# Attention ahead of an MLP and a mixture of experts: transposes by VectorE in squares of 32, value products with the keys' weights stationary, fronts three heads ahead

## The chip, the cores and the metric

The kernel runs on one core of one Trainium2 chip, as one program. The metric is the device time of one execution in microseconds; the profile's own clock counts from the start of its span. Engines are named as in the profile: PE is TensorE's stream of matmuls, PEld its loads of weights, DVE is VectorE, ACT is ScalarE, POOL is GpSimd, SP is SyncE, which here only issues DMAs.

## The reference

Softcapped attention over 2 batches of 12 heads with 448 tokens and 64 columns, then a squared-ReLU MLP over 896 tokens, then a mixture of 8 experts of which each token takes one:

```python
scores = scale * np.matmul(q, k.transpose(0, 1, 3, 2))
scores = cap * np.tanh(scores / cap)
scores = scores - np.max(scores, axis=-1, keepdims=True)
attn = np.exp(scores)
attn = attn / (np.sum(attn, axis=-1, keepdims=True) + 1e-09)
x = np.matmul(attn, v)              # then heads side by side: 896 x 768
...
h = x @ w_in                        # 768 x 2048
r = np.maximum(h, 0.0)
x = (r * r) @ w_out                 # 2048 x 768
...
expert_idx = np.argmax(xn @ en.T / tau, axis=1)
for e in range(E):                  # 8 experts, 768 x 1024 x 768
    mask = expert_idx == e
    h = np.maximum(x[mask] @ w1[e], 0.0)
    out[mask] = gate_w[mask, None] * (h @ w2[e])
```

The scores are not shifted by their maximum in the kernel; their cap of 30 bounds the exponential.

## The kernel before, in words

**Tiling.** Activations are kept transposed: partitions hold columns of the model, the free dimension the 448 tokens of a batch. A batch's tokens are cut into 4 blocks of 112 (`NC`, `CP`); token 4p + c stands in block c at place p. A head has 64 columns (`D`), so two heads, a pair, fill 128 partitions.

**Precision.** A float32 operand of the large products is written as the sum of two float32r parts, hi (rounded) and lo (the rest), and a product takes three passes: hi x hi, lo x hi, hi x lo (`pass3`, L450 to L452). Scores do it with stacked halves: `k_r` holds k twice beside each other, so that its transpose `kp` has k in both halves of the partitions; `kh` and `kl` are its hi and lo part. `q_s` holds q's hi part beside its lo part, so its transpose `q2` has q hi in partitions 0 to 63 and q lo in 64 to 127. Two passes of 128 partitions then make all products of a block of keys: kh with q2, and kl with q2. The products of p_t with v are plain float32, of which one product is two instructions in the trace.

**A head.** `front_k(n)` (GpSimd makes the hi and lo part of q in rows, L312 and L313; four transposes by TensorE, L317; a copy from PSUM, L320 by VectorE or L322 by ScalarE; a subtraction by VectorE, L324) and `front_q(n)` (four transposes by TensorE, L331; a copy from PSUM, L334 or L336) prepare k and q. `scores(n, hf)` makes half of the scores: for two blocks of keys two passes into a PSUM bank of 448 queries (L345, L346) and a tanh by ScalarE out of that bank (L347), then one exp over both (L348); `p_t` has keys on partitions and queries in the free dimension. `values(n)` makes four float32 products (L358): the weights are a block's 112 keys by 64 columns of v beside 64 columns of ones (`vt`), the moving operand is p_t with 448 queries. So one half of the bank `pv` receives the values, transposed as they are wanted, and the other half the sum over the keys, in 64 equal rows; ScalarE adds the guard and brings the sums to `den` (L367). `finish(m)`, for a pair of heads, takes the reciprocal of den (128 x 448, L386), multiplies (L389, twice) and leaves to `split_pair` the hi part `xh` by ScalarE (L383) and the lo part `xl` by VectorE (L384).

**Order.** The program is written as Python generators; every engine executes its own instructions in the order in which they were written, and waits for others by semaphores. The generator `attention()` goes through 24 heads. In its loop over n it writes: front_k(n+2), scores(n+1, 0), front_q(n+2), scores(n+1, 1), the conversion of a weight block, finish of the pair before, values(n). In the first batch (heads up to 12 of the loop) it runs alone: three banks take turns for scores, three for values, and `convert_early` makes VectorE turn four blocks of w_in from float64 to float32 along the way (L263, L169, L170, L172; a block every other head). Then `interleave(mlp(0), 192, att, ATN)` weaves it into the first MLP of batch 0: after every step of the MLP (three passes) as many steps of attention as `ATN` over 192 asks for. There two banks serve scores, two values, and two the MLP; the copies of `front_k` and `front_q` go to ScalarE (`eng["kh"]`). After that come the MLP of batch 1 with the router of batch 0, the experts, and one tile of tokens that were left over.

**Loads.** `load_head` is called for two heads ahead of the loop and once in every front_k. It issues k twice (into the two halves of k_r) and q on SP; `load_v` issues v of head n+2 after values(n). Pools give every tile a few buffers (k_r and q_r 2, p_t 4); a writer waits until the readers of the buffer's last use are done.

Of the kernel before, what the change touches and what calls it, by code (L numbers as in the profile page):

```python
# [8 lines left out]
F32 = mybir.dt.float32  # L9
# [4 lines left out]
ALU = mybir.AluOpType  # L14
# [6 lines left out]
def kernel(  # L21
# [37 lines left out]
    T = 64  # L59
    OOB = 4096.0  # L60
# [16 lines left out]
    # ---------------------------------------------------------------- heads  # L77
# [3 lines left out]
    vt = [ap.tile([CP, NC, 2, D], F32, tag=f"vt{i}", name=f"vt{i}", bufs=1) for i in range(2)]  # L81

    def load_head():
        n = nload[0]
        if n >= len(order):
            return
        nload[0] = n + 1
        b, h = order[n]
        q_r = ap.tile([CP, NC, D], F32, tag="q_r", name=f"q_r{n}", bufs=2)
        k_r = ap.tile([CP, NC, 2, D], F32, tag="k_r", name=f"k_r{n}", bufs=2)  # L90
        kk = k[b, h].rearrange("(p c) d -> p c d", c=NC)
        qq = q[b, h].rearrange("(p c) d -> p c d", c=NC)
        e = nc.sync if n else nc.scalar
# [3 lines left out]
        raw[n] = (q_r, k_r)  # L97

    def load_v(n):
        b, h = order[n]  # L100
        nc.sync.dma_start(vt[n % 2][:, :, h % 2, :], v[b, h].rearrange("(p c) d -> p c d", c=NC))
# [4 lines left out]
    # ------------------------------------------------------------ constants  # L106
# [6 lines left out]
    identr = const.tile([P, P], F32R, name="identr")  # L113
    nc.vector.tensor_copy(identr, ident)
    for i in range(2):
        nc.gpsimd.memset(vt[i][:, :, 1 - i, :], 1.0)
# [13 lines left out]
    # ------------------------------------------------------- weight streams  # L130
# [949 lines left out]
```

## Time and profile before

| | |
|---|---|
| runs of the kernel | 540.63, 540.63, 2953.97 us; median 540.63 |
| span of the profiled execution, within one of such time | 536.6 us |
| between the span and the median | 4.0 us |
| busy: PE, PEld | 520.5 us (97%), 439.6 us (82%) |
| busy: DVE, ACT, POOL | 388.2 us (72%), 308.1 us (57%), 39.2 us (7%) |
| instructions | 7614 |
| DMA | 87.88 MB in 110713 packets, 163 GB/s over the span |

The profile shows one execution. Busy time of an engine is the time in which at least one of its instructions ran. TensorE overlaps: a matmul is in flight while the next begins, so the length of one matmul is longer than the distance to the next, and the distance between starts tells the pace. In a row `xN` says how many instructions it stands for. A row ends with the idle time of the engine just before it and with what ended that. Shapes stand as partitions x elements, for matmuls as the weights' partitions*columns and then the moving operand.

### The profile page before, as it was taken

The page shows a single profiled execution, that of the slowest core. Times are in us where ns is not written, and L with a number is a line of the kernel's source. Part 1 is how long each engine was busy: PE and PEld are TensorE (multiplying, and loading weights), DVE is VectorE, ACT ScalarE, POOL GpSimd, SP SyncE. Part 2 cuts the span into 40 slices and gives each one's busy share as a digit, 9 for nine tenths or more (in the row PEclk, how much of TensorE's full clock was granted, in tenths as well). Part 3 has the DMA queues.
Part 4 walks back from the last instruction along what each step waited for, and adds up shares of the span by engine and source line. Part 5 has one row for each costly group of instructions (what it writes and reads, how often), then busy time and mean ns, then how long its engine had stood idle before and what let it go on. Part 6 is the DMA issues. An engine that isn't in the chain of part 4 may idle for free.

```text
span 536.6 us, 7614 instructions
## 1 busy us (share of the span) xinstructions
PE 520.5 (97%) x2550; PEld 439.6 (82%) x2550; DVE 388.2 (72%) x667; ACT 308.1 (57%) x562; POOL 39.2 (7%) x67
## 2 busy tenths in 40 slices
PE   6999998999999999999999999999999999999994
PEld 5666567888888888879999899999889898998992
DVE  4699999999979998889398666645548444546751
ACT  4999889888878678865433331222453233444530
POOL 3222212011101100000100000000000000000000
PEclk9999999999999999999999999999999999999998
DMA  6676668768666767675823213344712245644641
GB/s 171 172 201 169 184 165 234 240 216 258 197 192 178 240 183 247 202 234 164 271 91 119 76 61 117 99 149 139 188 41 79 81 132 169 197 154 151 215 135 38
DMA packets 110713, 87.88 MB, mean 164 GB/s; under 512 B 37442, under 2 KB 97346, under 8 KB 110672
## 3 DMA queue, kind: packets, MB, share of 16 engines
q1 hardware_dynamic: 101904, 81.92, 50.9%
q10 hardware_dynamic: 8672, 5.42, 3.7%
q8 instruction: 21, 0.34, 0.3%
q14 instruction: 20, 0.16, 0.1%
q0 software_dynamic: 96, 0.04, 0.0%
HBM read 69.43 MB, written 18.28 MB: 163 GB/s over the span
## 4 chain that ended last, share of the span: by engine, by line
PE 89%; DVE 6%; DMA 2%; ACT 1%; issue 0%; SPq 0%; DVEq 0%; ACTq 0%
PE pv L358 10%; PE h L450 7%; PE y L450 7%; PE y L451 7%; PE h L451 7%; PE y L452 7%; PE h L452 7%; PE z L450 4%; PE e L450 4%; PE z L451 4%; PE e L451 4%; PE z L452 4%; PE e L452 4%; PE sc L345 3%; PE sc L346 3%; DVE den L386 2%
## 5 line engine op out<-in xcount | busy, mean ns | idle before, releaser
L198 DVE TENSOR_TENSOR wl<-wf,wh 128x512 fp32r<-128x512 f32 (+1 forms) x140 | 110.4, 800 | 52.9 <-ACT wh L192 51.1
L192 ACT CAST wh<-wf 128x512 fp32r<-128x512 f32 (+1 forms) x97 | 65.8, 697 | 24.4 <-PE z L452 8.8
L358 PE MATMUL pv<-p_t,vt 112*128 112x448 f32 x192 | 78.1, 539 | 1.2 <-DVE den L389 1.2
L450 PE MATMUL h<-xh,wh 128*128 128x448 f32 x192 | 76.0, 396 | 0.0
L450 PE MATMUL y<-gh,wh 128*128 128x448 f32 x192 | 75.1, 391 | 0.0
L451 PE MATMUL y<-gh,wl 128*128 128x448 f32 x192 | 70.2, 366 | 0.0
L451 PE MATMUL h<-xh,wl 128*128 128x448 f32 x192 | 70.1, 365 | 0.0
L452 PE MATMUL h<-xl,wh 128*128 128x448 f32 x192 | 70.1, 365 | 0.0
L452 PE MATMUL y<-gl,wh 128*128 128x448 f32 x192 | 70.1, 365 | 0.0
L347 ACT ACTIVATE p_t<-sc,rcap 112x448 f32<-112x448 f32 x96 | 55.5, 629 | 6.3 <-PE sc L346 5.9
L358 PEld LDWEIGHTS pv<-p_t,vt 112*128 112x128 f32 x192 | 36.1, 189 | 25.9 <-issue 22.8
L348 ACT ACTIVATE p_t<-p_t,capb 112x896 f32<-112x896 f32 x48 | 50.1, 1044 | 1.6
L480 ACT ACTIVATE r<-h 128x448 f32<-128x448 f32 x32 | 17.3, 540 | 40.4 <-PE h L452 25.7
L450 PEld LDWEIGHTS h<-xh,wh 128*128 128x128 f32 x192 | 36.1, 188 | 5.2 <-issue 2.2
L345 PE MATMUL sc<-q,kh 128*112 128x448 f32 x96 | 38.4, 400 | 1.8 <-ACT p_t L347 1.8
L451 PEld LDWEIGHTS h<-xh,wl 128*128 128x128 f32 x192 | 36.2, 188 | 4.8 <-issue 2.2
L450 PEld LDWEIGHTS y<-gh,wh 128*128 128x128 f32 x192 | 36.1, 188 | 4.5 <-issue 1.9
L451 PEld LDWEIGHTS y<-gh,wl 128*128 128x128 f32 x192 | 36.2, 188 | 4.3 <-issue 1.9
L452 PEld LDWEIGHTS h<-xl,wh 128*128 128x128 f32 x192 | 36.1, 188 | 2.9
L452 PEld LDWEIGHTS y<-gl,wh 128*128 128x128 f32 x192 | 36.1, 188 | 2.9
L194 DVE CAST wh<-wf 128x512 fp32r<-128x512 f32 (+1 forms) x43 | 20.7, 481 | 23.6 <-PE y L452 19.5
L450 PE MATMUL z<-hh,wh 128*128 128x448 f32 x96 | 36.3, 379 | 0.0
(229 smaller groups left out, 943.4 us busy)
## 6 DMA issues: line engine op xcount, KB each, us to landing
wr<-in_moe_w_in_dram SPq DMA_DIRECT2D x16, 768.0 KB, 5.7
wr<-in_moe_w_out_dram SPq DMA_DIRECT2D x24, 512.0 KB, 4.7
wf<-in_moe_w_dram SPq DMA_DIRECT2D x24, 384.0 KB, 3.6
wf<-in_moe_w_dram SPq DMA_DIRECT2D x36, 256.0 KB, 3.1
wf<-wk SPq DMA_DIRECT2D x20, 384.0 KB, 3.8
wk<-wf SPq DMA_DIRECT2D x16, 384.0 KB, 2.9
wk<-wf SPq DMA_DIRECT2D x24, 256.0 KB, 2.6
wf<-wk SPq DMA_DIRECT2D x24, 256.0 KB, 2.9
```

Of the source, the lines that this page charges most:

```text
L192: nc.scalar.copy(c["hi"], c["f"])
L194: nc.vector.tensor_copy(c["hi"], c["f"])
L198: nc.vector.tensor_tensor(c["lo"], c["f"], f32(c["hi"]), op=ALU.subtract)
L345: nc.tensor.matmul(sc[:CP, :S], kh[:, c * CP:(c + 1) * CP], q2, start=True, stop=False)
L346: nc.tensor.matmul(sc[:CP, :S], kl[:, c * CP:(c + 1) * CP], q2, start=False, stop=True)
L347: nc.scalar.activation(p_t[:, j], sc[:CP, :S], AF.Tanh, scale=rcap[:CP])
L348: nc.scalar.activation(p_t, p_t, AF.Exp, scale=capb[:CP])
L358: nc.tensor.matmul(pv[:, :S], vv[:, c], pl[c // 2][:, c % 2], start=c == 0, stop=c == NC - 1)
L450: nc.tensor.matmul(o, wh, xh, start=first, stop=False)
L451: nc.tensor.matmul(o, wl, xh, start=False, stop=False)
L452: nc.tensor.matmul(o, wh, xl, start=False, stop=last)
L480: nc.scalar.activation(r, o[:, :S], AF.Relu)
```

## The change

**Transposes of q and k.** They leave TensorE. k and q of a head are loaded into one tile `qk` of 128 partitions by four DMAs, as squares of 32: partition 64 + 32j + t holds k, partition 32j + t holds q, of token 32s + t in square s, columns 32j to 32j + 31. VectorE's `transpose`, which turns each square of 32 x 32 in its place (L320, STREAM_TRANSPOSE in the trace), makes q transposed in partitions 0 to 63 and k transposed in 64 to 127 of `tq`. `kp` then holds k's lo part in partitions 0 to 63 and its hi part in 64 to 127 (a cast, L339 or L341 on ScalarE, and a subtraction, L323); `qh` holds q's hi part twice, `ql` zeros over q's lo part (a cast as above; GpSimd makes the second half of qh, L333, and the lo part, L334). The two passes of a block of keys, kp with qh and kp with ql, give the same three products (L350, L351); both have the same weights. k is loaded once.

**Value products.** The operands are swapped: p_t, a block of 112 keys by 112 queries, is the weights, and v with a column of ones, 65 columns, is moved (L364). For each of four blocks of queries four blocks of keys are summed up, 16 float32 products a head. The bank holds queries on partitions, 64 columns of values and one sum for each of four blocks. VectorE adds the guard, takes the reciprocal of 112 x 4 sums and multiplies (L375 to L377). `finish(m)` turns a pair's rows back by four transposes on TensorE (L393); ScalarE copies them from PSUM as xh (L394), VectorE makes xl (L395).

**Order.** The fronts go three heads ahead, behind both halves of the scores; finish stands in the middle of the next head's values; `convert_early` is split over two heads, behind the values; `ATN` is 72 in place of 78. Tokens stand as 112c + p in place of 4p + c, which also moves rows of the router and of the output.

```diff
-        q_r = ap.tile([CP, NC, D], F32, tag="q_r", name=f"q_r{n}", bufs=2)
-        k_r = ap.tile([CP, NC, 2, D], F32, tag="k_r", name=f"k_r{n}", bufs=2)
...
-        e.dma_start(k_r[:, :, 0, :], kk)
-        nc.sync.dma_start(k_r[:, :, 1, :], kk)
-        nc.sync.dma_start(q_r, qq)
+        qk = ap.tile([P, S // SQ, SQ], F32, tag="qk", name=f"qk{n}", bufs=3)
+        for i, a in enumerate((k, q)):
+            halves = a[b, h].rearrange("(s t) (j d) -> j t s d", t=SQ, d=SQ)
+            for j in range(2):
+                e = nc.scalar if n == 0 and j else nc.sync
+                o = (2 * (1 - i) + j) * SQ
+                e.dma_start(qk[o:o + SQ], halves[j])
...
         def front_k(n):
...
+            load_head()
+            tq = ap.tile([P, S], F32, tag="tq", name=f"tq{n}", bufs=2)
+            nc.vector.transpose(tq, qk.rearrange("p s d -> p (s d)"))
+            kp = ap.tile([P, S], F32R, tag="kp", name=f"kp{n}", bufs=2)
+            copy(kp[D:], tq[D:])
+            nc.vector.tensor_tensor(kp[:D], tq[D:], f32(kp[D:]), op=ALU.subtract)
+            st[n] = [tq, kp, []]
+
+        def front_q(n):
...
+            copy(qh[:D], tq[:D])
+            e = nc.gpsimd if n else nc.vector
+            e.tensor_copy(qh[D:], tq[:D])
+            e.tensor_tensor(ql[D:], tq[:D], f32(qh[:D]), op=ALU.subtract)
+            st[n][0] = (qh, ql)
...
         def scores(n, hf):
...
-                nc.tensor.matmul(sc[:CP, :S], kh[:, c * CP:(c + 1) * CP], q2, start=True, stop=False)
-                nc.tensor.matmul(sc[:CP, :S], kl[:, c * CP:(c + 1) * CP], q2, start=False, stop=True)
+                nc.tensor.matmul(sc[:CP, :S], kc, qh, start=True, stop=False)
+                nc.tensor.matmul(sc[:CP, :S], kc, ql, start=False, stop=True)
...
         def values(n):
...
-            for c in range(NC):
-                nc.tensor.matmul(pv[:, :S], vv[:, c], pl[c // 2][:, c % 2], start=c == 0, stop=c == NC - 1)
-                if c == 1:
+            for t in range(NC):
+                for c in range(NC):
+                    nc.tensor.matmul(pv[:, t], pl[c // 2][:, c % 2, t * CP:(t + 1) * CP], vt[n % 2][:, c],
+                                     start=c == 0, stop=c == NC - 1)
+                if t == 1:
                     yield
+                    if n >= 2 and n % 2 == 0:
+                        finish(n // 2 - 1)
...
-            nc.scalar.activation(den[D - z:2 * D - z], pv[z:z + D, :S], AF.Identity, bias=ecap[z:z + D])
+            nc.vector.tensor_scalar(rs, pv[:, :, D], ecap[:CP], None, op0=ALU.add)
+            nc.vector.reciprocal(rs, rs)
+            nc.vector.tensor_tensor(pair[n // 2][:, :, h % 2], pv[:, :, :D],
+                                    rs.unsqueeze(2).to_broadcast([CP, NC, D]), op=ALU.mult)
...
-            nc.vector.reciprocal(den, den)
-            for i in range(2):
-                o = slice(i * D, (i + 1) * D)
-                nc.vector.tensor_tensor(den[o], pair.pop(2 * m + i)[o, :S], den[o], op=ALU.mult)
-            todo.append(parts)
+            for c in range(NC):
+                nc.tensor.transpose(tp[:, c * CP:(c + 1) * CP], den[:, c].rearrange("p t d -> p (t d)"), ident[:CP, :CP])
+            nc.scalar.copy(xh[:, cc], tp)
+            todo.append(lambda: nc.vector.tensor_tensor(xl[:, cc], tp, f32(xh[:, cc]), op=ALU.subtract))
```

The order on TensorE for one head of attention alone, before. Each row is an instruction or a run of equal ones, with its line, the tile written and the tiles read; the number behind a name tells one tile from the next:

```order
L317 MATMUL kp_250<-ident,k_r_146 128x112 x4
L345 MATMUL sc_0_260<-q_220,kh_201 112x448
L346 MATMUL sc_0_260<-q_220,kl_203 112x448
L345 MATMUL sc_1_264<-q_220,kh_201 112x448
L346 MATMUL sc_1_264<-q_220,kl_203 112x448
L331 MATMUL qp_269<-identr,q_s_242 128x112 x4
L345 MATMUL sc_2_277<-q_220,kh_201 112x448
L346 MATMUL sc_2_277<-q_220,kl_203 112x448
L345 MATMUL sc_3_281<-q_220,kh_201 112x448
L346 MATMUL sc_3_281<-q_220,kl_203 112x448
L358 MATMUL pv_291<-p_t_0_205,vt_82 128x448 x2
L358 MATMUL pv_291<-p_t_1_222,vt_82 128x448 x2
```

And at the same place of the change, from the last block of a head's scores to the first of the next head's:

```order
L350 MATMUL sc_3_317<-qh_214,kp_211 112x448
L351 MATMUL sc_3_317<-ql_102,kp_211 112x448
L364 MATMUL pv_336<-vt_81,p_t_0_243 112x65 x2
L364 MATMUL pv_336<-vt_81,p_t_1_253 112x65 x2
L364 MATMUL pv_336<-vt_81,p_t_0_243 112x65 x2
L364 MATMUL pv_336<-vt_81,p_t_1_253 112x65 x2
L393 MATMUL xp_347<-ident,den_236 128x112 x4
L364 MATMUL pv_336<-vt_81,p_t_0_243 112x65 x2
L364 MATMUL pv_336<-vt_81,p_t_1_253 112x65 x2
L364 MATMUL pv_336<-vt_81,p_t_0_243 112x65 x2
L364 MATMUL pv_336<-vt_81,p_t_1_253 112x65 x2
L350 MATMUL sc_0_374<-qh_273,kp_270 112x448
```

The transposes of k and q are gone from between the scores, and the transposes of a finished pair (xp) stand between the two halves of the values.

VectorE for one pair of heads of attention alone, before: two rounds of kh, kl and the copy of q, a reciprocal with its two products between them, the lo part xl of the pair, and a weight block's four instructions:

```order
L320 CAST kh_311<-kp_306 128x448
L324 TENSOR_TENSOR kl_313<-kp_306,kh_311 128x448
L334 COPY q_330<-qp_325 128x448
L386 RECIPROCAL den_240<-den_240 128x448
L389 TENSOR_TENSOR den_240<-pv_234,den_240 64x448
L389 TENSOR_TENSOR den_240<-pv_291,den_240 64x448
L320 CAST kh_371<-kp_366 128x448
L324 TENSOR_TENSOR kl_373<-kp_366,kh_371 128x448
L334 COPY q_390<-qp_385 128x448
L384 TENSOR_TENSOR xl_346<-den_240,xh_345 128x448
L263 TENSOR_SCALAR wf_404<-wr_232 128x768
L169 TENSOR_SCALAR wf_404<-wf_404 128x768
```

And there in the change, one head with the second half of a weight block and the lo part of a pair:

```order
L320 STREAM_TRANSPOSE tq_327<-qk_204 128x448
L339 CAST kp_329<-tq_327 64x448
L323 TENSOR_TENSOR kp_329<-tq_327,kp_329 64x448
L339 CAST qh_332<-tq_327 64x448
L375 TENSOR_SCALAR rs_363<-pv_336,ecap 112x4
L376 RECIPROCAL rs_363<-rs_363 112x4
L377 TENSOR_TENSOR den_362<-pv_336,rs_363 112x4x64
L175 SCALAR_TENSOR_TENSOR wf_299<-wr_168,wf_299 128x768
L177 SCALAR_TENSOR_TENSOR wf_299<-wr_168,wf_299 128x768
L395 TENSOR_TENSOR xl_346<-xp_347,xh_345 128x448
```

A head's normalisation now follows its own values, on 4 sums a partition in place of 448, and the front's four operations stand ahead of it.

TensorE in the first MLP with attention woven in, before, between the two halves of a head's scores (sc), with the MLP's passes (h):

```order
L345 MATMUL sc_1_1156<-q_1014,kh_974 112x448
L346 MATMUL sc_1_1156<-q_1014,kl_976 112x448
...
L452 MATMUL h_3_1116<-xl_346,wh_959 128x448
L331 MATMUL qp_1173<-identr,q_s_1122 128x112 x4
L450 MATMUL h_4_1186<-xh_345,wh_1026 128x448
...
L452 MATMUL h_4_1186<-xl_346,wh_1026 128x448
L345 MATMUL sc_2_1200<-q_1014,kh_974 112x448
```

And in the change:

```order
L350 MATMUL sc_1_1039<-qh_921,kp_914 112x448
L351 MATMUL sc_1_1039<-ql_101,kp_914 112x448
L450 MATMUL h_0_1028<-xh_345,wh_845 128x448
...
L452 MATMUL h_0_1028<-xl_346,wh_845 128x448
L350 MATMUL sc_2_1058<-qh_921,kp_914 112x448
```

Before, 15 passes of the MLP and four transposes of q lay between the halves; in the change it is 9 passes.

## Rows read from the trace of the kernel before

**Rows 1.** Table by stretches: length, busy us (instructions) of PE, PEld, DVE, ACT, POOL; clock; DMA.

```profile
14.10:85.10 71.00, 67.98 (x297) 44.12 (x297) 64.04 (x79) 64.98 (x94) 16.21 (x24) 1.00 0.69 182
85.10:240.30 155.20, 155.20 (x732) 127.66 (x731) 140.78 (x201) 126.03 (x222) 13.53 (x16) 1.00 0.71 218
```

**Rows 2.** Timeline of PE, one head of attention alone: start, length, line, operands.

```profile
22.48 0.55 PE L317 MATMUL kp<-ident,k_r 112*128 112x112 f32 x4
22.79 0.43 PE L345 MATMUL sc<-q,kh 128*112 128x448 f32 x1
23.07 0.36 PE L346 MATMUL sc<-q,kl 128*112 128x448 f32 x1
23.27 0.36 PE L345 MATMUL sc<-q,kh 128*112 128x448 f32 x1
...
24.85 3.17 PE L358 MATMUL pv<-p_t,vt 112*128 112x448 f32 x8
27.86 0.55 PE L317 MATMUL kp<-ident,k_r 112*128 112x112 f32 x4
```

**Rows 3.** Waits from 14.1 to 85.1: engine, line, releaser, total us, times, longest.

```profile
PE sc L345 <- ACT p_t L347: 1.8, 1, 1.8
...
PE pv L358 <- DVE den L389: 1.2, 2, 0.9
```

**Rows 4.** Timeline of PEld, about 420 us, then about 521 us.

```profile
419.60 1.01 PEld L747 LDWEIGHTS mp<-meta,sm 112*64 112x64 f32 x16 [0.31 <-issue]
420.62 0.19 PEld L450 LDWEIGHTS z<-hh,wh 128*128 128x128 f32 x1
420.73 0.19 PEld L451 LDWEIGHTS z<-hh,wl 128*128 128x128 f32 x1
...
521.15 0.92 PEld L887 LDWEIGHTS xm<-ys,smt 64*112 64x112 f32 x8 [0.30 <-issue]
```

**Rows 5.** Costliest groups, shapes apart: count, busy us, mean ns, idle before.

```profile
L347 ACT ACTIVATE p_t<-sc,rcap 112x448 f32<-112x448 f32 x96 | 55.5, 629 | 6.3 <-PE sc L346 5.9
L348 ACT ACTIVATE p_t<-p_t,capb 112x896 f32<-112x896 f32 x48 | 50.1, 1044 | 1.6
L386 DVE RECIPROCAL den<-den 128x448 f32<-128x448 f32 x12 | 35.3, 2945 | 0.6 <-ACT den L367 0.6
...
L170 DVE SCALAR_TENSOR_TENSOR wf<-wr,wf 128x768 int32<-128x768 int32 x16 | 15.4, 963 | 0.5
L389 DVE TENSOR_TENSOR den<-pv,den 64x448 f32<-64x448 f32 x24 | 14.9, 622 | 0.8
L468 DVE CAST gh<-r 128x448 fp32r<-128x448 f32 x32 | 13.0, 405 | 9.7 <-ACT r L465 9.7
...
L887 PEld LDWEIGHTS xm<-ys,smt 64*112 64x112 f32 x16 | 1.8, 172 | 0.6 <-issue 0.6
L747 PEld LDWEIGHTS mp<-meta,sm 112*64 112x64 f32 x16 | 1.0, 138 | 0.3 <-issue 0.3
L663 DVE RECIPROCAL gate<-gate 112x4 f32<-112x4 f32 x2 | 0.4, 178 | 0.1
```

**Rows 6.** Durations of two lines: ns minimum/median/maximum, first and last start in us.

```profile
L263 DVE TENSOR_SCALAR wf<-wr x4: 549/554/1086, 19.4 to 55.2; 128x768 f32<-128x768 f32 x4
...
L313 POOL TENSOR_TENSOR q_s<-q_r,q_s x23: 726/750/1336, 6.8 to 183.5; 112x256 fp32r<-112x256 f32 x23
```

**Rows 7.** Timeline about 197 us, attention woven into the MLP.

```profile
195.60 0.36 PE L346 MATMUL sc<-q,kl 128*112 128x448 f32 x1
...
198.98 1.15 ACT L347 ACTIVATE p_t<-sc,rcap 112x448 f32<-112x448 f32 x2
199.66 0.45 PE L345 MATMUL sc<-q,kh 128*112 128x448 f32 x1
```

**Rows 8.** Timeline of PE at the start.

```profile
8.18 0.57 PE L345 MATMUL sc<-q,kh 128*112 128x448 f32 x1
8.55 0.57 PE L346 MATMUL sc<-q,kl 128*112 128x448 f32 x1
```

More of the change, by code (lines that the diff above doesn't have):

```diff
@@ L80 @@
     nload = [0]
-    vt = [ap.tile([CP, NC, 2, D], F32, tag=f"vt{i}", name=f"vt{i}", bufs=1) for i in range(2)]
+    vt = [ap.tile([CP, NC, D + 1], F32, tag=f"vt{i}", name=f"vt{i}", bufs=1) for i in range(2)]
     def load_head():
@@ L112 @@
     make_identity(nc, ident)
-    identr = const.tile([P, P], F32R, name="identr")
-    nc.vector.tensor_copy(identr, ident)
+    qlo = [ap.tile([P, S], F32R, tag=f"ql{i}", name=f"ql{i}", bufs=1) for i in range(2)]
     for i in range(2):
-        nc.gpsimd.memset(vt[i][:, :, 1 - i, :], 1.0)
+        nc.gpsimd.memset(f32(qlo[i][:D]), 0.0)
+    for i in range(2):
+        nc.gpsimd.memset(vt[i][:, :, D:], 1.0)
     rcap = const.tile([P, 1], F32, name="rcap")
@@ L253, in convert_early @@
         i, odd = divmod(step, 2)
-        if not odd:
+        if odd and i < len(early):
+            c = early[i]
+            c["f"] = w_tile("wf", 1000 + i, c, 4, F32)
+            nc.vector.tensor_scalar_mul(c["f"], c["parts"][:, :, :, 1].bitcast(F32), 2.0 ** -112)
+            c["narrow"] = narrow(c)
+            c["narrow"][0]()
+        elif not odd:
             if 0 < i <= len(early):
                 c = early[i - 1]
+                for step in c["narrow"][1:]:
+                    step()
                 nc.sync.dma_start(c["keep"](), c["f"])
@@ L259, in convert_early @@
                 raw_w(early[i + 1], 1001 + i)
-        elif i < len(early):
-            c = early[i]
-            c["f"] = w_tile("wf", 1000 + i, c, 4, F32)
-            nc.vector.tensor_scalar_mul(c["f"], c["parts"][:, :, :, 1].bitcast(F32), 2.0 ** -112)
-            for step in narrow(c):
-                step()
     def add_mlp_chunks(b):
@@ L319, in front_k, with copy @@
+        def copy(o, i):
             if eng["kh"] == "dve":
[L320 removed]
+                nc.vector.tensor_copy(o, i)
             else:
[L322 to L337 removed]
+                nc.scalar.copy(o, i)
@@ L409, in attention @@
         yield
+        front_k(2)
+        yield
+        front_q(2)
+        yield
         for n in range(N):
-            due = n >= 2 and n % 2 == 0
-            if due and n > H:
-                finish(n // 2 - 1)
-                yield
-            if n + 2 < N:
-                front_k(n + 2)
-                yield
             if n + 1 < N:
@@ L420, in attention @@
                 yield
-            if n + 2 < N:
-                front_q(n + 2)
-                yield
-            split_pair()
-            if n + 1 < N:
                 scores(n + 1, 1)
                 yield
+            if n + 3 < N:
+                front_k(n + 3)
+                yield
+                front_q(n + 3)
+                yield
+            yield from values(n)
             if n <= H:
                 convert_early(n)
-            if due and n <= H:
-                finish(n // 2 - 1)
-            yield from values(n)
+            split_pair()
             yield
             if n == H:
-                split_pair()
                 yield "batch"
```

67 lines of the change are left out of this document (20 added, 47 removed).

## The prediction

> **What bounds the kernel now.** I read the table by stretches first (busy time of each engine in each). The program has a start, attention alone on the first batch (14.1 to 85.1 us, stretch A below), attention on the second batch woven into the first MLP (85.1 to 240.3, stretch B), and the rest, which the change does not touch except for the order of tokens. In B TensorE's busy time equals the stretch, 155.20 of 155.20 us; in A it is 67.98 of 71.00, with VectorE at 64.04 and ScalarE at 64.98 close behind [rows 1]. So in B only TensorE work counts, and in A a head is bound by TensorE with the other two near enough to take over.
>
> A busy TensorE need not be a working one, so I read TensorE's timeline over one head of A, start by start [rows 2]; the reader is to see that each row begins where the work before it ends. From one kp to the next is 5.38 us (22.48 to 27.86). The eight value passes take 3.01 (24.85 to 27.86; four float32 products are eight instructions). Scores step by 0.20, eight make 1.6. What is left, 0.77, is the eight transposes of q and k. ScalarE needs for a head four tanh of 0.63, two exp of 1.04 [rows 5] and one sum as long as a tanh: 5.2. The waits of TensorE in A, from the view of waits, are 1.8 on a score bank that a late tanh held and 1.2 on the normalised sums [rows 3]. Check: 13 values (39.1), 12 heads of scores (19.2), 13 heads of transposes (10.0) and 3.0 of waits make 71.3 against 71.0.
>
> **The change part by part, TensorE first.** Transposes of q and k: 0.77 a head go, 13 heads in A (10.0 us), 9 in B (6.9), two in the start.
>
> Value products: now 16 float32 products of 65 moving columns a head, two instructions each, 32 instead of 8. The moving columns fall from 448 to 65, and 3.01 x 65/448 x 4 would be 1.74 us. But each of the 32 loads other weights, 112 columns of p_t. The trace has weight loads that follow each other with almost nothing to stream: 16 loads of 64 columns for 4 moving columns [rows 4] take 1.01, the last one 0.138 long [rows 5], so (1.01 - 0.14)/15 = 0.058 each; two loads of 128 columns stand 0.11 apart (420.62, 420.73) [rows 4]. Between them, 112 columns come to 0.058 + 0.052 x 48/64 = 0.097. So 32 x 0.097 = 3.10 a head, against 3.01: the swap of the operands gives TensorE nothing, it costs 0.1 a head. That is the term I trust least. Its bounds: 0.054 (the moving columns decide, 1.74 a head) and 0.107 (the eight loads of 112 columns with 128 moving ones, (0.92 - 0.17)/7 [rows 4, 5], 3.42 a head). I take 0.097, since the loads of 64 show that a load does not wait for the stream before it, and since loads alone set that pace.
>
> [...]
>
> New transposes: a pair's normalised rows are turned back by four transposes of the same form as kp. kp takes 22.48 to 22.79, and the score behind it is drawn out by 0.08 (22.79 to 23.07, then 0.20 to 23.27) [rows 2], 0.39 a pair: six pairs in A (2.3), six in B (2.3).
>
> So A: 13 x 3.10 + 12 x 1.6 + 2.3 = 61.8 against 71.0, 9.2 less if nothing waits. B: 6.9 - 11 x 0.1 - 2.3 = 3.5 less.
>
> **The other engines.** VectorE before, per head, from the costliest groups: three PSUM operations of 448 columns (kh, kl, the copy of q) as long as the product with the reciprocal, 0.62, that product, half of a reciprocal of 2.945 and half a split of 0.62: 4.3 us [rows 5]. After: the transpose by squares, two casts of 64 x 448, one subtraction, two operations on 112 x 4, one product of 112 x 256 from PSUM, half a split. The casts are SBUF to SBUF, 0.405 in a like row; the subtraction and the product at most 0.62; the small ones 0.18 [rows 5]. The transpose is not in the trace: below, 0.405 (the cast of as many columns); above, 2.945 (the reciprocal, the slowest row of that shape). I take 0.62, being nearest in kind to one pass over 448 columns. Sum: 0.62 + 0.81 + 0.62 + 0.36 + 0.45 + 0.31 = 3.2. The weight conversion on top is four instructions of 768 columns a pair of heads before and after (split in halves now), two at 0.55 [rows 6] and two at 0.96 [rows 5], 3.0, so a head costs VectorE about 4.7 against 5.0 of TensorE. That is close, and why I do not give A its whole gain. ScalarE loses the sum of 0.63 per head and keeps the rest: 4.6. It hides behind 5.0.
>
> GpSimd gets 64 x 448 where it had 112 x 256, 1.75 times the columns: 1.3 for the subtraction (median 0.750 [rows 6]) and under 1 for the copy, 2 to 2.3 a head of its 5. It is hidden, unless it blocks VectorE (a rival).
>
> DMA: a head's k is loaded once and not twice, in pieces of 32 floats. Four issues of k and q replace three, one more per head on SP, to whose queue the chain of work that ended last gives no share. The loads run two fronts ahead of their use, some 10 us, and the queue is asked for them before the wait of v, as before; I cost them at nothing. If that cover went, the next front would be late and VectorE first to wait, but scores have one more head in hand.
>
> What stands behind waits: the finish of a pair now sits in the middle of the next head's values and needs den of the head before; VectorE has 1.6 + 1.5 us of TensorE work for two small operations and a product (0.8). kp of head n+3 waits for scores n+1 in the same buffer; behind it stands nothing that is due in that head. Both at nothing, and in A +1.0 in all for the moments when conversion lands on them.
>
> In B the two halves of a head's scores come closer: the transpose step between them is gone, and about 2.6 us instead of 4.2 lie from the first score to the third, which takes the bank of the first. Normally ScalarE starts the tanh at once; but once it was 3 us late (scores at 195.60, tanh at 198.98, the third score at 199.66 [rows 7]). There a wait of some 1.4 us comes up. I take +1.0 for B; below 0, above 3 (two such heads).
>
> Start: the first score needs transpose, cast, subtraction, cast, copy, subtraction on VectorE, some 3 us behind the landing instead of transposes and three operations: level with now within 0.5. [...]
>
> **Sum.** A -9.2 + 1.0, B -3.5 + 1.0, start +1.0: -9.7 on a span of 536.6, 526.9. The median shown is 540.63, 4.0 above the span; I add the same: **531 us**, 1.8% faster.
>
> **The rivals.** *VectorE and GpSimd get into each other's way, and A is bound by them.* For: a conversion step that takes 549 ns has been 1086, and GpSimd's subtraction 726 at best and 1336 at worst [rows 6]; VectorE now works from SBUF to SBUF where it read PSUM, and has 0.3 a head to spare. A block of 0.7 a head puts A at 5.4 a head, what it has now: the gain there is lost, about 538. Against: fronts three heads ahead can absorb several us. [...]
>
> *Weight loads run at 0.107:* 24 x 32 x 0.010 = +7.7, 539. The row for it has more to stream than the new products, so I hold it less likely.
>
> *Moving columns decide after all* (0.054): B gains 11 x 1.36 = 15 more, A can gain only until ScalarE's 4.6, about 5: 511. Against: 16 loads with four columns to stream still took 0.058 each.
>
> *Slower: TensorE falls to its lower level in the values.* There weights load and little streams, while now every stretch of A streams 448 columns. At the start's pace scores cost 0.17 more each, loads about 0.1 more: 1.4 + 3.1 = 4.5 a head. All of A at it would be 590; it decides from (551.4 - 531)/4.5, five heads. Nothing in the trace shows a warm stretch of that kind longer than a microsecond, either way.
>
> *Slower: the transpose costs like the reciprocal.* 2.3 more a head, VectorE 7.0 a head, A +2 x 13: 557. From 1.7 us per transpose on the time is over 551.
>
> **How the numbers follow.** The sum's own case 0.55, with a range of 526 to 537 (all three allowances nil and loads at 0.095: 526; the allowances at their upper ends: 537); VectorE with GpSimd 0.20 (538); loads at 0.107 0.08 (539); moving columns 0.05 (511); the clock 0.07 (560 to 590); the dear transpose 0.05 (557). 2% is about what a measurement of this kernel can tell from no change: 529.8 and 551.4. Faster: 0.05 and a good 0.28 of the first case, 0.33; slower: 0.12; within 2%: 0.55. The range 524 to 541 leaves out the clock, the transpose and the moving columns, 0.17.
>
> **What would show it.** Right: the 768 value instructions stand 0.095 to 0.10 apart; stretch A is about 63 us and a head 5.0; VectorE's reciprocal group is gone, its busy time lower by some 20 us; in B TensorE stays without idle. Wrong: a pitch of 0.055 or 0.11 for L364; waits of TensorE on den or on kp and qh in A (VectorE is the bound); scores stepping by 0.37 behind values (the clock); a STREAM_TRANSPOSE far over 0.62.

## The result, and the profile after

The changed kernel takes 547.1 us (median of four, 544.8 to 549.1) against 540.6; the ratio of the fast runs alone, which leaves out the run of 2954 us, is 1.0144, interval [1.0105, 1.0183]. It is slower, by less than the 2% that the prediction takes for no change; 531 us were forecast. The profiled execution, the quickest of the four, has a span of 542.8 us against 536.6, and 2.0 us lie around it.

The table by stretches, with the bounds at the first value product, at the first MLP pass and, as in [rows 1], 2.9 us ahead of the MLP's fourth set of x2t transposes (columns as there):

```profile
13.90:86.10 72.20, 68.11 (x537) 62.09 (x536) 61.70 (x118) 59.60 (x85) 25.51 (x27) 0.95 0.70 161
86.10:247.20 161.10, 154.68 (x948) 142.09 (x948) 130.89 (x221) 116.25 (x206) 14.97 (x16) 0.99 0.68 202
```

Attention alone (A) takes 72.2 us in place of 71.0 [rows 1]. In the woven part (B) TensorE had no idle time before; now 6.4 us of it are idle. That set of x2t transposes stands at 243.2 before and at 250.1 now; behind it nothing is lost (292.7 us left against 293.4). So all of it lies in A and B.

The values of a head came out as forecast, the scores 0.26 us longer. TensorE's timeline over one head in A, to hold against [rows 2], with one row of its weight loads (PEld):

```profile
39.32 3.27 PE L364 MATMUL pv<-vt,p_t 112*112 112x65 f32 x32
42.40 0.43 PE L350 MATMUL sc<-qh,kp 128*112 128x448 f32 x1
42.67 0.36 PE L351 MATMUL sc<-ql,kp 128*112 128x448 f32 x1
...
43.76 0.17 PEld L350 LDWEIGHTS sc<-qh,kp 128*112 128x112 f32 x1 [0.30 <-ACT p_t L352]
...
44.26 1.70 PE L364 MATMUL pv<-vt,p_t 112*112 112x65 f32 x16
```

The 32 value instructions step over 3.08 us (39.32 to 42.40), 0.096 each; scores take 1.86 (42.40 to 44.26). What went wrong stands at the end of A. Here three engines' timelines about it: SP issues the refill of a buffer from DRAM (L187) and a weight block (L165), ScalarE converts the block (L191) and then makes tanh (L352), TensorE makes scores (L350):

```profile
69.27 0.34 SPq L187 DMA_DIRECT2D wf<-wk  x1
69.66 0.44 SPq L165 DMA_DIRECT2D wr<-in_moe_w_in_dram  x1
...
72.21 1.04 ACT L353 ACTIVATE p_t<-p_t,capb 112x896 f32<-112x896 f32 x1
77.24 0.89 ACT L191 ACTIVATE wf<-wr 128x768 f32<-128x768 f32 x1 [3.98 <-DMA qk<-in_q_dram]
78.03 1.15 ACT L352 ACTIVATE p_t<-sc,rcap 112x448 f32<-112x448 f32 x2
...
78.70 0.71 PE L350 MATMUL sc<-qh,kp 128*112 128x448 f32 x1 [4.09 <-ACT p_t L352]
...
79.59 3.11 PE L364 MATMUL pv<-vt,p_t 112*112 112x65 f32 x16
```

ScalarE is done with the exp at 73.3 and stands until 77.2 in front of a weight block that has not landed; the tanh behind it is late, and TensorE waits 4.09 for the tanh's bank. The name of the DMA in brackets is that of the last one to report, a load of q; that the block itself was what ScalarE needed is seen from the DMA issues of that moment: issued at 69.66, it landed 7.4 us later, at 77.1.

```profile
wr<-in_moe_w_in_dram SPq DMA_DIRECT2D x1, 768.0 KB, 7.4
```

And TensorE comes back at half its clock (table by stretches; the granted clock is the third column from the end):

```profile
39.30:74.50 35.20, 35.20 (x291) 31.79 (x289) 33.45 (x64) 30.14 (x43) 12.29 (x13) 1.00 0.78 187
74.50:78.70 4.20, 0.11 (x1) 0.00 (x0) 1.47 (x5) 1.46 (x3) 1.12 (x1) 0.99 0.54 89
78.70:88.90 10.20, 10.20 (x46) 9.66 (x47) 8.54 (x14) 6.24 (x9) 1.87 (x2) 0.50 0.50 120
```

For 10.2 us the granted clock is 0.50; scores step by 0.37 there (87.75, 88.12), not by 0.20. Two score passes, a head's values and four transposes took 7.4 us there (78.70 to 86.11) where they take 0.5 + 3.1 + 0.4 at the full clock, 3.4 less; 1.4 more is lost on the first passes of B. The same pair of waits, ScalarE's conversion on a late block and the scores on a late tanh, comes again in B. In the waits view of the whole execution one wait of 4.1 and the 4.0 on qk are those of A; the rest lies in B. The last two lines are TensorE's timeline and the table by stretches at the longest wait of B:

```profile
PE sc L350 <- ACT p_t L352: 10.1, 4, 4.1
ACT wf L191 <- DMA qk<-in_q_dram: 4.0, 1, 4.0
ACT wf L191 <- DVE xl L395: 2.9, 1, 2.9
ACT wf L191 <- DMA wr<-in_moe_w_out_dram: 2.3, 1, 2.3
ACT wf L191 <- DMA wr<-in_moe_w_in_dram: 1.8, 2, 1.6
...
216.81 0.46 PE L350 MATMUL sc<-qh,kp 128*112 128x448 f32 x1 [3.00 <-ACT p_t L352]
216.80:220.00 3.20, 3.19 (x17) 2.73 (x18) 3.08 (x6) 3.14 (x5) 0.00 (x0) 1.00 0.81 270
```

B's three waits on tanh are 1.6, 1.3 and 3.0 us, and ScalarE stood 1.6, 2.3 and 2.9 in front of a block just ahead of them. The 2.9 is put down to VectorE's xl; the block had been asked for at 211.07, landed 3.9 later, and ScalarE started at 215.04. Behind the wait of 3.0 the granted clock is 1.00: not every wait of that length brings it down.

Sum against before: start -0.2; A +1.2 (a forecast of -8.2, and 4.1 of wait, 3.4 of clock and 1.9 of a head's pace over it); B +5.9 (idle time 6.4, of which 6.0 on tanh, clock 1.4, less 1.9 saved); the rest -0.7: +6.2, the difference of the spans.

### The profile page after: what moved, and what is told of

Same layout as the page of the kernel before. It is cut to its first block, busy times and chain, and to the rows that moved or that the text cites. A ratio compares the mean times of both kernels' runs of the same rounds, so it can differ in the third digit from the quotient of the medians.

```text
span 542.8 us, 8527 instructions
## 1 busy us (share of the span) xinstructions
PE 516.7 (95%) x2982; PEld 468.0 (86%) x2982; DVE 375.1 (69%) x728; ACT 291.9 (54%) x536; POOL 49.6 (9%) x69
## 2 busy tenths in 40 slices
DMA packets 129917, 85.19 MB, mean 157 GB/s; under 512 B 59330, under 2 KB 116546, under 8 KB 129872
## 4 chain that ended last, share of the span: by engine, by line
PE 74%; DVE 10%; ACT 5%; DMA 5%; issue 3%; SPq 2%; POOL 0%; DVEq 0%; ACTq 0%
PE pv L364 7%; PE y L450 6%; PE y L451 6%; PE y L452 6%; PE h L450 6%; PE h L452 5%; PE h L451 5%; PE z L450 4%; PE e L450 4%; PE z L451 4%; PE e L451 4%; PE e L452 4%; PE z L452 4%; DMA wr<-in_moe_w_in_dram 2%; PE sc L350 2%
## 5 line engine op out<-in xcount | busy, mean ns | idle before, releaser
L203 DVE TENSOR_TENSOR wl<-wf,wh 128x512 fp32r<-128x512 f32 (+1 forms) x140 | 109.7, 795 | 63.2 <-ACT wh L197 61.6
L364 PEld LDWEIGHTS pv<-vt,p_t 112*112 112x112 f32 x768 | 83.9, 183 | 1.7 <-PE sc L350 0.2
L364 PE MATMUL pv<-vt,p_t 112*112 112x65 f32 x768 | 83.5, 265 | 0.0
L450 PE MATMUL h<-xh,wh 128*128 128x448 f32 x192 | 72.0, 375 | 0.5 <-ACT r L480 0.5
L450 PE MATMUL y<-gh,wh 128*128 128x448 f32 x192 | 71.9, 375 | 0.0
L352 ACT ACTIVATE p_t<-sc,rcap 112x448 f32<-112x448 f32 x96 | 55.4, 626 | 17.7 <-PE sc L351 17.5
L350 PE MATMUL sc<-qh,kp 128*112 128x448 f32 x96 | 39.4, 411 | 17.5 <-ACT p_t L352 10.1
L350 PEld LDWEIGHTS sc<-qh,kp 128*112 128x112 f32 x96 | 17.6, 183 | 25.9 <-ACT p_t L352 16.1
```

Of the source, the lines that this page charges most:

```text
L203: nc.vector.tensor_tensor(c["lo"], c["f"], f32(c["hi"]), op=ALU.subtract)
L350: nc.tensor.matmul(sc[:CP, :S], kc, qh, start=True, stop=False)
L352: nc.scalar.activation(p_t[:, j], sc[:CP, :S], AF.Tanh, scale=rcap[:CP])
L364: nc.tensor.matmul(pv[:, t], pl[c // 2][:, c % 2, t * CP:(t + 1) * CP], vt[n % 2][:, c], start=c == 0, stop=c == NC - 1)
L450: nc.tensor.matmul(o, wh, xh, start=first, stop=False)
```

## The experiments

Theory **W**: scores wait on tanh because ScalarE, in order, stands in front of a weight block that landed late, and the clock falls behind the longest of these waits. Rival **L**: GpSimd and VectorE block each other, and VectorE is what is late. Rival **V**: the value products lower the clock by themselves. All runs, with the time, the ratio to the kernel before in the same group, and the granted clock of the profiled execution:

| run | us | ratio [95%] | clock |
|---|---|---|---|
| e1 conversion one block later | 529.4 | 0.982 [0.978, 0.985] | 0.996 |
| e3 halves of scores apart in B | 538.8 | 1.000 [0.998, 1.003] | 0.995 |
| h1 fronts only | 576.9 | 1.070 [1.067, 1.073] | 0.962 |
| h2 values only | 548.5 | 1.017 [1.015, 1.020] | 0.997 |
| e13 = e1 and e3 | 530.0 | 0.982 [0.977, 0.988] | 0.996 |
| e1b before, with e1's edit | 537.1 | 0.996 [0.994, 0.998] | 0.995 |
| h1b fronts only, mended | 563.3 | 1.043 [1.039, 1.048] | 0.976 |
| e12 = e1 without GpSimd | 536.5 | 0.996 [0.992, 0.999] | 0.985 |
| a0 the change again | 547.1 | 1.012 [1.005, 1.018] | 0.987 |
| e4 = e1, two heads ahead | 546.2 | 1.010 [1.004, 1.016] | 0.984 |
| ga = e1, pauses in values | 545.5 | 1.012 [1.009, 1.016] | 0.970 |
| gb = e1, short pauses in scores | 533.1 | 0.985 [0.980, 0.991] | 0.997 |
| va1 = e1, pauses in values by GpSimd | 547.5 | 1.016 [1.012, 1.021] | 0.980 |
| sc3 = e1, long pauses in scores | 552.7 | 1.025 [1.022, 1.028] | 0.965 |

**e1: give a weight block's load two blocks' time.**

```diff
-    AHEAD = {"load": 7, "conv0": 6, "conv1": 5, "store": 4, "split": 3}
+    AHEAD = {"load": 7, "conv0": 5, "conv1": 5, "store": 4, "split": 3}
```

> The changed kernel, with one number changed: ScalarE's conversion of a weight block (L191) is asked for one block later, so that its load has two blocks' time in place of one. Theory W (scores wait 10.1 us on tanh because ScalarE stands before a weight block that landed late, and TensorE falls to its lower level after the longest of these waits): the 4.1 us wait at the end of attention alone goes, the clock there stays at 1.00, and of the 5.9 us in the woven part about half goes; 8 to 12 us less than the changed kernel, 535 to 539 us. Rival L (GpSimd and VectorE block each other, and VectorE is what is late): the waits stay, 545 us or more. Rival V (the value products of 65 columns lower the clock by themselves): the wait goes, but a stretch at half clock stays, 541 to 545.

529.4 us, below the expected 535 to 539 and 1.8% faster than before. Three executions lie at 529.1 to 529.5; a fourth, not profiled, took 539.6 at a clock of 0.976. Stretches A and B, B here up to the fourth set of x2t, and ScalarE and SP at the end of A:

```profile
13.78:78.45 64.67, 64.67 (x537) 58.70 (x536) 57.93 (x114) 57.13 (x82) 24.39 (x26) 1.00 0.73 170
78.45:234.17 155.72, 155.09 (x963) 144.16 (x963) 137.56 (x232) 119.23 (x212) 16.68 (x17) 1.00 0.75 218
...
68.14 0.43 SPq L165 DMA_DIRECT2D wr<-in_moe_w_in_dram  x1
...
76.97 1.04 ACT L353 ACTIVATE p_t<-p_t,capb 112x896 f32<-112x896 f32 x1
77.92 0.91 ACT L191 ACTIVATE wf<-wr 128x768 f32<-128x768 f32 x1
```

The block is asked for at 68.14 and needed at 77.9; ScalarE no longer waits for it, TensorE is busy through all of A, and no stretch of A or B is at half clock. The same number also asks for the refills (L187) one block later, and the load took 6.0 us in place of 7.4. The shorter load alone would by estimate have left a wait of 1 us: it landed at 74.1, and ScalarE was free of the exp before at 73.1. The span, 527.5, is near the forecast's 526.9. W stands, L and V fall as causes of the loss.

**e3: the halves of the scores apart in B.** `values(n)` is started between `scores(n+1, 0)` and `scores(n+1, 1)` for n > H:

```diff
+            g = values(n)
+            if n > H:
+                next(g)
+                yield
...
-            yield from values(n)
+            yield from g
```

> The changed kernel; in the part woven into the MLP the first half of a head's value products stands between the two halves of the next head's scores (attention alone is as it was). Theory W with bunching (in the woven part four tanh and two exp come as one block of ScalarE, weight blocks come late behind it): the waits of scores on tanh in the woven part, 5.9 us, fall to 1 to 3; the wait at the end of attention alone stays; 542 to 545 us. If bunching has nothing to do with it (late weight blocks alone, or rival L): waits there stay at 4 or more, 546 to 549.

538.8 us, below the expected 542 to 545. All waits of scores in B are gone (6.0 before the edit); A keeps one:

```profile
PE sc L350 <- ACT p_t L352: 2.3, 1, 2.3
```

In the profiled execution the clock stayed at 1.00 behind it, and that one took 532.3; most others have a clock of 0.982 to 0.988 and 536 to 540 us. So the late block is not enough in B: it costs when the next scores follow at once. Either edit, the earlier block or the distance, takes the waits away, and both together give no more:

> Both edits on the changed kernel: conversion of a weight block one block later, and in the woven part the halves of the scores apart. Theory W says that each of them alone takes away the same waits in the woven part (neither profile had one left there), so together they give no more than the later conversion alone: 527 to 531 us. If bunching costs more than its waits (VectorE and ScalarE late elsewhere), 522 to 526.

530.0 us: as expected under W.

**e1b: the same edit on the kernel before.**

> The kernel before, with the same number changed (conversion of a weight block one block later), and nothing of the change. Theory W: its only wait of that kind is 1.8 us at the end of attention alone, so it gains 1 to 3 us: 536 to 538. The change is then worth 7 to 10 us on equal terms. If most of the gain of the later conversion belongs to the weight stream, whatever the attention, 529 to 533.

537.1, as expected: its A goes from 71.0 to 68.6 us, and the longest wait of scores on tanh is 0.5 in place of 1.8. All ten executions have a clock of 0.995 to 0.997; of the kernel before, nine of 19 in that group have 0.989 to 0.992. On equal terms the change is worth 7.7 us (529.4 against 537.1): 4.0 of it in A, 2.2 in B.

**h1 and h2: each part alone.** h1 has the new fronts with the old value products, sums and reciprocal; h2 the new values with the old fronts.

> One part of the change alone: fronts by VectorE's transposes, three heads ahead, order of tokens, split conversion; value products, sums by ScalarE and the pair's reciprocal as before (finish ahead of the values, 78 steps). TensorE needs 4.6 us a head in attention alone (3.0 + 1.6), ScalarE 5.2. Theory W: ScalarE bounds attention alone at 5.2 to 5.4 a head, VectorE (reciprocal back) at 5.5 to 6 may bound it; the woven part loses 6.9 us of transposes but keeps late weight blocks and bunched scores: 534 to 542. Rival V (the 65-column products cost the clock): no stretch at half clock behind the start, 530 to 535.

> The other part alone: value products with p_t stationary and a column of ones, small sums on VectorE, transposes of the finished pair; fronts by TensorE, two heads ahead, between the halves of the scores, as before (72 steps). TensorE needs 5.7 us a head in attention alone (5.38 + 0.1 + 0.2), 4 us more in all, and 3.4 more in the woven part; ScalarE is lighter by 0.63 a head. Theory W: no new waits of scores on tanh, since the weight blocks keep their distance from the scores; 545 to 549 us. Rival V: stretches at half clock in or behind value products, 550 or more.

h1, 576.9, missed by far. Its waits:

```profile
PE sc L350 <- ACT p_t L352: 24.9, 16, 5.5
```

I took the cause to be the place of the pair's split, behind the values, where ScalarE would stand until the reciprocal is through. h1b puts it between the halves of the scores, as before, and has e1's edit:

> Fronts alone again (value products, sums and reciprocal as before), with two things moved that spoilt its first form: the split of a finished pair stands between the halves of the scores, as in the kernel before, and weight blocks are converted one block later. Expected if the first form lost its time to ScalarE standing before the pair's reciprocal: the 3 us waits of every other head go; VectorE bounds attention alone at about 6 us a head while it converts weights (2.2 front, 2.4 half a reciprocal with its products, 1.5 conversion), 5.2 by ScalarE after; the woven part gains up to 6.9: 530 to 538. If the fronts and the old normalisation do not go together at all (VectorE in order is too late for both): 550 or more.

563.3: the second case of the expectation, the fronts and the old normalisation don't go together in this order. VectorE's and TensorE's timelines over a pair:

```profile
40.27 2.94 DVE L391 RECIPROCAL den<-den 128x448 f32<-128x448 f32 x1
43.24 1.28 DVE L394 TENSOR_TENSOR den<-pv,den 64x448 f32<-64x448 f32 x2
...
43.96 3.25 PE L363 MATMUL pv<-p_t,vt 112*128 112x448 f32 x8 [2.88 <-DVE den L394]
```

The reciprocal of 2.94 stands behind four front operations in VectorE's order, and TensorE waits 2.9 for the bank that it frees, twice, and a third time 3.0 for what the profile does not name. A is 79.9 us long at a clock of 0.91, 8.9 more than before. Another 14.7 us are lost behind A, where scores wait up to 4.9 on tanh; their cause was not followed. h2, 548.5, lies in the expected range, in part by waits that were not expected:

```profile
PE qp L331 <- DVE kl L324: 5.3, 5, 1.1
```

A takes 77.8 us there, 6.9 more than before where 4 was expected; 5.3 of it are waits for VectorE's kl. So neither part pays alone in the orders tried: the value products cost TensorE time, but free VectorE of 1.3 us a head (half of 2.94 + 1.28, against 0.82 for the small sums and the product) and ScalarE of its sum. That this is what the new fronts need is argued from h1b's VectorE in A; for B it is not shown.

**e12: rival L directly.** On e1, VectorE does GpSimd's two operations (`e = nc.vector`).

> The changed kernel with the later conversion, and q's second hi half and lo part made by VectorE in place of GpSimd, so that GpSimd does nothing in attention. Rival L (the two block each other): VectorE's long operations (L175 up to 1.77 us, the subtraction L323 at 0.86) shorten to 0.96 and 0.62, VectorE stays under TensorE's 5.0 a head; 524 to 529. Theory W: VectorE gets 1.0 a head more (4.7 to 5.3 with conversion) and is just above TensorE in attention alone, blocked time given back in part: 529 to 535.

Groups of VectorE with shapes apart, and TensorE about 58 us with the stretch behind:

```profile
L175 DVE SCALAR_TENSOR_TENSOR wf<-wr,wf 128x768 int32<-128x768 int32 x16 | 15.3, 956 | 0.4
L323 DVE TENSOR_TENSOR kp<-tq,kp 64x448 fp32r<-64x448 f32 x24 | 14.9, 621 | 5.6 <-ACT kp L341 5.0
...
58.23 0.60 PE L393 MATMUL xp<-ident,den 112*128 112x112 f32 x4 [0.96 <-DVE den L377]
...
59.30:73.00 13.70, 13.70 (x59) 12.62 (x59) 10.24 (x22) 6.33 (x10) 0.00 (x0) 0.50 0.63 144
```

The block between the two is real: in e1 the same groups mean 1143 and 760 ns. But it was hidden, and without GpSimd VectorE comes late: 536.5, 1.5 above the range of W (executions from 534.5 to 542.2). A wait of 0.96 us among value products was followed by 13.7 us at half clock.

**e4: fronts two heads ahead, on e1.**

> The changed kernel with the later conversion of weight blocks, and the fronts two heads ahead in place of three. VectorE and GpSimd need about 4 us (transpose to ql) from front_k to the scores that read it, and only one head's values, 3.1 us of TensorE, lie between. Expected if three heads ahead is what hides the front: scores wait on ql or qh about 1 to 2 us a head in attention alone, 13 heads, and TensorE pauses there; 545 to 565. If it is spare: 529 to 531 as with three heads.

546.2. Waits in A, and the scores behind a head's values:

```profile
PE sc L351 <- POOL ql L334: 4.1, 5, 1.0
PE sc L350 <- DVE rs L375: 2.9, 4, 0.8
...
34.12 0.42 PE L350 MATMUL sc<-qh,kp 128*112 128x448 f32 x1 [0.48 <-DVE rs L375]
35.30 0.48 PE L351 MATMUL sc<-ql,kp 128*112 128x448 f32 x1 [0.76 <-POOL ql L334]
35.60 0.55 PE L350 MATMUL sc<-qh,kp 128*112 128x448 f32 x1
```

Three heads ahead is needed: VectorE and GpSimd come late with two, up to a microsecond, on five heads of A. The time is in the expected range, but not by 1 to 2 us on 13 heads: the waits are 7.0 us and the loss 16.8, since the clock in A is 0.91. Behind each of the four pairs of waits it fell (a mean of 0.56 from 35.3 to 38.0, behind the pair shown), behind the fifth head's single 1.04 it did not.

**The change again, and pauses put in.** Is the wait at the end of A chance, and does the clock fall by it?

> The changed kernel as it is, once more, beside the others of this group, to see whether the wait at the end of attention alone and the half clock behind it come in every execution. Theory W: the scores' wait there is 2 to 4.5 us (the load lands 5.6 to 7.4 us after its issue), the clock over the whole execution lies between 0.98 and 0.99, 543 to 549 us. If both were chance, some profile shows no such wait and 532 to 538.

```profile
PE sc L350 <- ACT p_t L352: 10.2, 4, 4.5
...
79.29 0.89 ACT L191 ACTIVATE wf<-wr 128x768 f32<-128x768 f32 x1 [4.43 <-DMA wr<-in_moe_w_in_dram]
```

The wait comes again, 4.5 us, with half clock behind it, and here the bracket names the weight block itself, which landed 7.8 us after its issue. On e1 I then put three pauses each into A: a transpose that nothing uses and that waits for small copies by VectorE (ga), for a tanh (gb), or for memsets by GpSimd (va1, sc3, whose edit follows):

```diff
+            zp = ps.tile([P, S], F32, tag="tr", name=f"zp{n}", bufs=2)
+            nc.tensor.transpose(zp[:CP, :CP], zt[:, :CP], ident[:CP, :CP])
+            for _ in range(reps):
+                nc.gpsimd.memset(zt[:, :w], 1.0)
+            nc.tensor.transpose(zp[:CP, CP:2 * CP], zt[:, :CP], ident[:CP, :CP])
```

> The changed kernel with the later conversion (529 us) and three pauses of TensorE of about 1 us put in, each in the middle of a head's value products (heads 3, 7 and 11: a transpose, not used, that waits for two small copies by VectorE). Theory C (a stretch of 65-column value products around a pause lets the clock fall): behind two or three of the pauses TensorE runs at half clock for 5 to 14 us, granted clock of the execution 0.96 to 0.98, 540 to 555. Rival: a pause costs its length alone, 531 to 534.

> The same with three pauses of about 1 us between the halves of the scores of heads 4, 8 and 12 (a transpose, not used, that waits for the second tanh). Theory C (it takes the value products around the pause, not the pause): clock as without pauses, 0.996; 531 to 535. Rival (any pause of this length in attention alone can bring the clock down): stretches at half clock behind these pauses too, 538 or more.

> The changed kernel with the later conversion and three short pauses of TensorE among value products (heads 3, 7 and 11, behind 12 of a head's 16 products: a transpose, not used, that waits for one memset by GpSimd of a tile that the transpose ahead of it read; about 0.9 us each, as long as the pauses that cost only their length among the scores). Theory C (the place decides: value products around a pause let the clock fall): behind at least one of three TensorE is at half clock, 535 to 545, the runs apart by several us. Theory D (the length decides: pauses of 2.5 us and more bring the clock down wherever they stand, short ones don't): clock 0.996, 531 to 534.

> The same kernel with three long pauses, about 2.7 us, between the halves of the scores of heads 4, 8 and 12 (five memsets in place of one). Theory C: the pauses cost their length and no more, since scores of 448 columns stand on both sides, clock 0.99 or more, 536 to 539. Theory D: half clock behind them as behind the pauses of 2.5 to 3.2 us among the value products, clock 0.97 to 0.98, 543 to 552.

Two of four were not the pauses I meant: VectorE and GpSimd had other work ahead, and those in ga lasted 2.5 to 3.2 us, those in va1 2.9 to 3.6. sc3 and gb came as planned. Of sc3 the first pause and the stretch behind it, then the same of va1, then gb up to 78 us, then the start of ga, ahead of its first pause:

```profile
28.10:30.90 2.80, 0.06 (x1) 0.00 (x0) 2.77 (x5) 1.79 (x3) 2.36 (x5) 0.99 0.20 49
30.90:41.20 10.30, 10.28 (x45) 9.55 (x46) 4.01 (x10) 3.76 (x6) 1.68 (x2) 0.51 0.63 156
...
31.30:34.60 3.30, 0.07 (x1) 0.00 (x0) 1.43 (x3) 0.66 (x1) 2.20 (x3) 0.97 1.00 297
34.60:41.10 6.50, 6.47 (x27) 5.91 (x28) 3.88 (x9) 3.59 (x6) 0.55 (x1) 0.50 0.53 91
...
14.00:78.00 64.00, 61.48 (x501) 55.73 (x501) 52.99 (x108) 52.74 (x76) 22.18 (x25) 1.00 0.68 157
...
13.40:23.80 10.40, 10.40 (x49) 9.70 (x49) 4.30 (x10) 6.04 (x9) 3.49 (x4) 0.52 0.47 89
```

Behind each of the nine long pauses TensorE is at half clock for 3 to 12 us, among scores as among values, so C, that the value products must stand around it, fell; behind none of gb's three, 0.84 each, is it. In time over e1: sc3 23.3 us for 9.0 us of pauses, va1 18.1 for 9.8, ga 16.1 for 8.5, gb 3.7 for 2.5. A pause of about 3 us in A cost 5 to 8. But D, that length alone decides, fell too: 0.96 us sufficed in e12 and pairs of 0.5 to 0.8 in e4, both next to value products, while five waits of 1.1 in h2, behind scores, did nothing (1.00 in its A), and the waits of 3.0 in B of the change, 3.4 in B of its repeat and 2.3 in e3 left the clock at 1.00. In ga's profile the clock fell at 13.4 us, with waits of 0.65 and 0.70 some 2 us ahead, where e1 with 0.52 and 0.55 kept it; so ga's 0.970 is not all due to its pauses. What exactly tips it stays open.

## Why the prediction was wrong, point by point

**Value products: right.** 0.096 us an instruction against 0.097, by the loads in [rows 4, 5], and 3.08 a head against 3.10. The moving columns (0.054) and the wider load (0.107) are excluded.

**Scores: 1.86 a head, not 1.6.** I took 0.20 from step to step and booked the 0.08 by which a score behind other work is drawn out to the transposes; it stays behind values. At the fourth block two more steps are long, 0.28 and 0.29, and there the load of weights waits 0.30 for the bank of the first tanh, 12 times in e1's A; before, the transposes of q stood between. 0.26 on 12 heads is 3.1 us, which the allowance of 1.0 in A did not hold: e1's A is 64.7 us (13.78 to 78.45) where 62.8 was forecast.

**The new work on the other engines: right.** The transpose by squares takes 636 ns (0.62 taken), VectorE 3.4 a head (3.2), GpSimd 1.9 (2 to 2.3), a pair's transposes 0.39. VectorE's busy time fell by 13.1 us (388.2 to 375.1), not by some 20. The block between VectorE and GpSimd was there, as that rival had it (L323 takes 750 ns, in e12 beside an idle GpSimd 621), and stayed covered.

```profile
L334 POOL TENSOR_TENSOR ql<-tq,qh 64x448 fp32r<-64x448 f32 x23 | 27.8, 1209 | 36.5 <-ACT qh L341 15.5 <-DVE qh L339 9.4 <-DVE rs L375 6.6
L323 DVE TENSOR_TENSOR kp<-tq,kp 64x448 fp32r<-64x448 f32 x24 | 18.0, 750 | 9.3 <-ACT kp L341 8.8
L320 DVE STREAM_TRANSPOSE tq<-qk 128x448 f32<-128x448 f32 x24 | 15.3, 636 | 4.3 <-DMA qk<-in_q_dram 4.3
```

**The step that failed: the wait in [rows 3].** I read that scores waited 1.8 us on a late tanh, and let the wait vanish from the sum ("9.2 less if nothing waits") without asking what had made the tanh late. Before, too, it was a weight block. SP's and ScalarE's timelines of the kernel before, and the issue's time to landing:

```profile
74.07 0.42 SPq L160 DMA_DIRECT2D wr<-in_moe_w_in_dram  x1
...
78.44 0.63 ACT L367 ACTIVATE den<-pv,ecap 64x448 f32<-64x448 f32 x1
80.47 0.90 ACT L186 ACTIVATE wf<-wr 128x768 f32<-128x768 f32 x1 [1.40 <-DVE kl L324]
...
wr<-in_moe_w_in_dram SPq DMA_DIRECT2D x1, 768.0 KB, 6.3
```

It was issued at 74.07 and landed at 80.4, and ScalarE, free since 79.1, started at 80.5. (The bracket names VectorE's kl, which ended at 80.4 too, but the conversion reads nothing of it.) ScalarE came to its block 5.0 us after the issue then, and 3.6 after it in the change: a head is shorter, and SP, which waits in order for a buffer that VectorE's split (L203) frees, issues L187 only at 69.27 (L203 ends at 69.24) and the block behind it. And the load took 7.4 in place of 6.3. That makes 1.4 and 1.1 of the 2.6 us by which ScalarE's wait grew; why the load itself took longer was not tried. A rival is the loads of q and k in pieces of 32 floats: the execution has 59330 packets under 512 B in place of 37442. The prediction costed loads of q and k at nothing and did not look at those of the weights, whose steps are tied to the steps of attention: a faster head leaves them less time.

**B's allowance: +1.0, at most 3; it was 6.4 of waits.** The mechanism named there, halves closer together and a late tanh, is half of it: more distance takes the waits away (e3), but so do earlier blocks with the halves as close as they are (e1), and the late blocks were not in it. The price was taken from one late tanh in the trace of before, 1.4; three came, of 1.6, 1.3 and 3.0.

**The clock: the rival was there, with the wrong trigger.** I had it fall in the values themselves, to the pace of the start (scores step by 0.37, [rows 8]), by five heads, at a chance of 0.07. In e1's profile it never falls in A or B. In the change it fell to 0.50 behind a wait of 4.1, and that cost 4.8 more. As the price of a wait, which may come or not, it belonged into the first case, not into a rival.

The forecast's own case, 526 to 537, is what e1 does at 529.4. It was a forecast of the change without the stall that it ran into. That e1's span comes within 0.6 us of the forecast's is in part luck: its A gains 6.3 us where 8.2 were forecast, its start 0.3 where 1.0 was to be lost; B, 2.4 less against 2.5, came out. No run shows the +1.0 of the start: the first value product stands at 14.10 before, at 13.90 in the change, where TensorE waits 0.53 and 0.69 on its way there, and at 13.78 in e1.

Three figures of the prediction are off, and none decides. It adds 4.0 us from span to time, where all executions of which both are recorded have 1.7 to 2.4 between them; its span of 526.9 stands for about 529. With allowances of 1.0 in A, 3 in B and 3 at the start the range ends at 535, not 537. And a dear transpose reaches 551 by its own steps at about 2.5 us, not 1.7.

## What to carry to other kernels

A wait that the profile shows before a change is a term: follow it to the instruction that stands ahead of the releaser in its engine's order, and ask whether what it waits for is timed by the work that is about to become faster. Where loads are issued a fixed number of steps ahead, shorter steps mean later loads, and one block's more distance was worth 17.7 us here. And two parts of a change can each lose alone (9 us for the values, 24 for the fronts) and win together; that one frees the engine which the other loads is the likely reason, shown in part.

## What the runs showed of the hardware

Nine pauses of TensorE of 2.5 to 3.6 us, put into attention alone (ga, va1, sc3), cost 5 to 8 us each on average, because the granted clock then stood at 0.50 for 3 to 12 us; in sc3 it came back at 41.1 us for a pause that ended at 30.9, behind a half of the scores, a head's values and most of the next head's scores. Waits of 3.0 us (the change) and 3.4 (its repeat) in the woven part cost no clock: it stood at 1.00. Float32 weights of 112 columns with 65 moving columns went at 0.096 us an instruction in the change. A transpose by squares of 128 x 448 float32 on VectorE took 0.64 there, a cast of 64 x 448 from SBUF 0.38 to 0.39 with GpSimd idle (e12), and a subtraction of that size 0.62 with GpSimd idle (e12) and 0.75 beside it (the change).
